# Retention attention and two feed-forward layers: the first four chunks of attention taken as whole chunks, and a new order for the first block

## The chip, the cores and the metric

The kernel runs on one core of a Trainium2 chip. The metric is the device time of one execution in microseconds (us); lower is better. A time is compared with the median of several executions of the kernel before.

## The reference, cut to what matters

```python
scores = scale * np.matmul(q, k.transpose(0, 1, 3, 2))          # B, H, S, D = 4, 8, 576, 64
gamma = 1.0 - 2.0 ** (-5.0 - np.arange(H))
Dmat = np.where(rel >= 0, gamma[:, None, None] ** rel, 0.0)     # rel = query position - key position
x = np.matmul(scores * Dmat, v)                                 # -> x of 2304 tokens x 512
h = x @ moe_w_in;  x = np.maximum(0.01 * h, h) @ moe_w_out      # 512 -> 2048 -> 512
h = x @ moe2_w_in; out = (h * np.cos(h)) @ moe2_w_out
...
```

There is no softmax. The decay is a power of gamma, so that it is split into factors on q, k, v and the result, and what is left of the mask is 0 or 1. Everything is float32.

## The kernel before, in words

**Tiles and stages.** The 2304 tokens are 18 chunks of 128. The feed-forward layers work on blocks of tokens; the first layer has five blocks (512, 512, 512, 384, 384 tokens), and block 0 is chunks 0 to 3. Each product of the feed-forward layers is three products of rounded parts (high times low, low times high, high times high, the type fp32r), so every weight and every input is first split into a high and a low part.

**Weights.** The layer's weights arrive as 64-bit words (1 MB for each of the 16 slices `f` of 128 hidden units) and are turned into float32 by a chain: on ScalarE `abs` (L552) and `lo` (L556), on VectorE `cs` (clamp and shift, two instructions, L560 and L562), `or` (L569) and `add` (L576), then `hi` (ScalarE, L585) and `low` (VectorE, L588). Slice 0 is done in two halves, `a` and `b`.

**Attention.** A chunk's load `ch` (L301) brings q and k transposed by heads, k and v by tokens. `sq` (L315) and `sv` (L327 on VectorE, L322 on ScalarE) scale q and v. Before the change every chunk is done as two halves of 64 tokens: `s` computes k·q within each half (L363), `m` masks it (L384, one VectorE instruction of 128x512), `v` multiplies by the values (L401), `g` makes k times v of each half (L425), `st` adds it to the running state (L449, one per half), `r` multiplies the state before each half by q (L464), and `tk` scales the result into `xr` (L503). Then `xh` and `xl` (L600, L604) split it into high and low, and the first feed-forward matmul can start.

**Feed-forward.** `H0.0` to `H15.3` are the input products of block 0 (L616, 12 matmuls for each of 16 slices), `O0` to `O15` the output products (L630, 12 each). `lk`, `gh`, `gl` (L641, L646, L651) are what lies between. `V3` to `V7` are "visits": the matmuls of attention for the chunks of block 1, put between those of block 0. `~n` are filler matmuls of n times 128 columns, on data that nobody reads (L522).

**What sets the order.** All of block 0 stands in a list written out by hand, `FIRST` (L53 to L71). Each word is a step, and a step's instructions go to their engines' queues in the list's order; each engine (and SyncE's queue of DMA issues, SP) takes its own in that order. All later work has its order in another list, `SECOND`, with the same content before and after. Three loads have an added wait: the first chunk of block 1 (ch4) and slices 2 and 3 wait for chunk 3's `g`, slice 1 and the second half of slice 0 for chunk 1's `s` (`raw()` in `step`, `load_chunk`). With `rows_done` the next group of matmuls in the same banks waits for an empty GpSimd instruction (POOL, L350), which waits for the group before.

Of the kernel before, what the change touches and what calls it, by code (L numbers as in the profile page):

```python
# [68 lines left out]
lk14 gh14 gl14 st8.1 tk7 H15.0 H15.1 H15.2 H15.3 O14 lk15 or15b add15b gh15 gl15 hi15b low15b O15 m8 ch9 sq9
sv9  # L70
# [168 lines left out]
def retention_ffn_ffn(  # L239
# [28 lines left out]
    def scratch(name, shape):  # L268
# [27 lines left out]
    def load_chunk(i):  # L296
        if 2 <= i < n_first:

            ch = w_tile(NF + 1 - i, [P, 4, DM], F32, "ch")
        else:  # L300
            ch = ap.tile([P, 4, DM], F32, tag="ch", name="ch")  # L301
        ch_t[i] = ch
        if i == 0:
            nc.sync.dma_start(ch[:, :2], qkv[i, :2].rearrange("x p d -> p x d"))
            nc.sync.dma_start(ch[:, 2:], qkv[i, 2:].rearrange("x p d -> p x d"))
        else:
            got = nc.sync.dma_start(ch, qkv[i].rearrange("x p d -> p x d"))
            if i == n_first:
                in_turn(got, last_of["grown"])
# [23 lines left out]
    def banks_of(i):  # L333

        if i < n_first:
            b = (6, 4, 0, 2)[i]
            lo, hi = [(b, 0), (b + 1, 0)], [(b, NP * C), (b + 1, NP * C)]
            return lo, hi, lo
# [17 lines left out]
    def scores(i):  # L356
        s, ch = banks_of(i)[0], ch_t[i]
        for p in range(NP):
            for x in range(2):
                for e, r in enumerate(halves):  # L360
# [6 lines left out]
                        start=i < n_first or p == 0 and (e == 0 or i == n_first),  # L367
# [3 lines left out]
                    if i >= n_first and e and ("part", i - 1) in last_of:  # L371
                        in_turn(got, last_of.pop(("part", i - 1)))
                    last_of["pe", i - 1] = got
        last_of["scores", i] = got

    def masks(i):
        b, o = banks_of(i)[0][0]
        if i < n_first:

            pt = w_tile(NF // 2 - 1 - i, [P, 2, NP, C], F32, "p_sb")  # L380
        else:
            pt = ap.tile([P, 2, NP, C], F32, tag="p", name="p_sb", bufs=1)
        p_t[i] = pt
# [6 lines left out]
        if i >= n_first:  # L390
            in_turn(got, last_of["pe", i - 1])

    def values(i):
        v, ch, pt = banks_of(i)[1], ch_t[i], p_t.pop(i)
        first = True
        for p in range(NP):
            for x, tok in enumerate(halves):
                for e, r in enumerate(halves):
# [10 lines left out]
                    if first and i >= n_first:  # L409
# [4 lines left out]
        last_of["values", i] = got  # L414

    def growth(i):
        n, ch = banks_of(i)[2], ch_t[i]
        for p in range(NP):
            for x, tok in enumerate(halves):
                if tokens_of(i)[x] == SUBS - 1:  # L420
                    continue
                for e, r in enumerate(halves):
# [6 lines left out]
                        start=i >= n_first and p == 0 and (x == 0 or i == n_first),  # L429
# [3 lines left out]
        last_of["grown"] = got  # L433
# [19 lines left out]
    def reads(i, part):  # L453
# [3 lines left out]
        for p in range(NP):  # L457
            for e, r in enumerate(halves):
# [15 lines left out]
                if ("st", i) in last_of and i < n_first:  # L474
                    in_turn(last_of["pe", i], last_of.pop(("st", i)))
# [1132 lines left out]
```

## Time and profile before

| what | us |
|---|---|
| median of 3 runs | 829.0 (828.11 to 830.35) |
| profiled execution, its own time | 829.85 |
| its span, first to last instruction | 827.7 |
| TensorE busy in the span | 809.1 (98%) |
| VectorE, ScalarE busy | 643.1 (78%), 540.1 (65%) |
| mean granted TensorE clock | 0.991 |

Times in the rows are microseconds from the span's start. The profiled execution is 0.85 us over the median. Its profile shows the engine's matmul rows (PE) and weight-load rows (PEld) apart; a float32 matmul has two rows of each.

### The profile page before, as it was taken

What the parts mean: (1) busy time and instruction counts of PE and PEld (TensorE: products, weight loads), DVE (VectorE), ACT (ScalarE), POOL (GpSimd) and SP (SyncE); (2) the same over time, 40 slices, a digit from 0 to 9 for tenths busy, and PEclk for the clock granted to TensorE, in tenths of its full rate; (3) what the DMA queues carried; (4) which work ended last, traced back from release to release, by engine and by line L of the source; (5) the groups of instructions that cost most, each with busy time, mean ns of one, the idle gap of its engine ahead of it and who ended that gap; (6) DMA issues with size and microseconds to landing.
All of it is one profiled execution on the core that took longest, in us unless ns stands there. A gap on an engine that the chain in (4) does not pass through costs nothing.

```text
span 827.7 us, 16049 instructions
## 1 busy us (share of the span) xinstructions
PE 809.1 (98%) x6134; PEld 742.6 (90%) x6134; DVE 643.1 (78%) x1148; ACT 540.1 (65%) x1041; POOL 6.1 (1%) x8
## 2 busy tenths in 40 slices
PE   7899999999999999999999989999999999999997
PEld 4678887888888888999999989999899999999997
DVE  5899987888887868777741278798698888888785
ACT  4788866556555556466432488887678876778861
POOL 0000011000000000000000000000000000000000
PEclk8899999999999999999999999999999999999999
DMA  8774616786878677867689287598848896637644
GB/s 322 261 275 153 230 53 204 255 256 211 296 250 252 241 228 255 259 221 223 206 265 406 91 349 283 205 331 308 357 132 295 318 384 266 226 127 274 250 164 168
DMA packets 101308, 203.78 MB, mean 246 GB/s; under 512 B 9072, under 2 KB 54896, under 8 KB 96112
## 3 DMA queue, kind: packets, MB, share of 16 engines
q1 hardware_dynamic: 101088, 202.41, 69.0%
q8 instruction: 48, 0.79, 0.4%
q10 hardware_dynamic: 144, 0.35, 0.2%
q14 instruction: 28, 0.23, 0.1%
HBM read 147.42 MB, written 55.31 MB: 245 GB/s over the span
## 4 chain that ended last, share of the span: by engine, by line
PE 80%; DMA 7%; DVE 6%; issue 3%; ACT 2%; SPq 1%; DVEq 0%; POOLq 0%; ACTq 0%
PE psum L630 20%; PE psum L616 20%; PE psum L1435 19%; PE psum L1263 18%; DMA wp<-wp 3%; DMA ch<-in_qkv 1%; DMA y<-graw 1%; DMA ws<-ws 1%; PE psum L401 1%; DMA raw<-in_w 1%; PE psum L464 1%; PE psum L425 1%; DVE t L569 1%; DVE t L576 1%; DVE w L588 1%
## 5 line engine op out<-in xcount | busy, mean ns | idle before, releaser
L616 PE MATMUL psum<-x_sb,w 128*128 128x512 f32 (+1 forms) x960 | 212.0, 370 | 1.2 <-DVE x_sb L604 0.9
L630 PE MATMUL psum<-g,w 128*128 128x512 f32 (+1 forms) x960 | 211.8, 370 | 0.4 <-DVE graw L873 0.4
L616 PEld LDWEIGHTS psum<-x_sb,w 128*128 128x128 f32 x960 | 174.8, 188 | 26.1 <-DVE x_sb L604 1.6
L630 PEld LDWEIGHTS psum<-g,w 128*128 128x128 f32 x960 | 174.4, 188 | 25.3 <-DVE g L651 1.4
L1263 PE MATMUL psum<-x,ws 128*128 128x384 f32 x576 | 111.3, 337 | 2.8 <-DMA ws<-ws 2.3
L1263 PEld LDWEIGHTS psum<-x,ws 128*128 128x128 f32 x576 | 101.5, 189 | 3.5 <-DMA ws<-ws 2.6
L917 DVE TENSOR_TENSOR g<-graw,g 128x512 fp32r<-128x512 f32 (+1 forms) x64 | 39.7, 623 | 61.0 <-ACT g L914 60.8
L1435 PE MATMUL psum<-g,wp 128*128 128x384 f32 x432 | 83.1, 338 | 2.8 <-DMA wp<-wp 1.9
L1263 PE MATMUL psum<-x,wa 128*128 128x384 f32 x432 | 84.0, 335 | 0.0
L1435 PE MATMUL psum<-g,wq 128*128 128x384 f32 x432 | 80.9, 335 | 0.1
L1435 PEld LDWEIGHTS psum<-g,wp 128*128 128x128 f32 x432 | 75.7, 189 | 4.7 <-DMA wp<-wp 1.9
L1435 PEld LDWEIGHTS psum<-g,wq 128*128 128x128 f32 x432 | 75.2, 188 | 0.9 <-DVE acc L1472 0.7
L1263 PEld LDWEIGHTS psum<-x,wa 128*128 128x128 f32 x432 | 75.7, 188 | 0.0
L910 ACT ACTIVATE graw<-psum 128x512 f32<-128x512 f32 (+1 forms) x64 | 34.7, 542 | 60.7 <-PE psum L616 56.1
L914 ACT CAST g<-graw 128x512 fp32r<-128x512 f32 (+1 forms) x64 | 36.1, 567 | 48.0 <-PE psum L630 47.8
L1472 DVE TENSOR_TENSOR acc<-psum,acc 128x384 f32<-128x384 f32 x90 | 48.3, 553 | 19.9 <-PE psum L1435 19.5
L1312 DVE SCALAR_TENSOR_TENSOR r<-r,h 128x768 f32<-128x768 int32 x48 | 45.6, 954 | 6.8 <-ACT r L1307 6.3
L1293 DVE TENSOR_TENSOR h<-psum,s 128x384 f32<-128x384 f32 x48 | 26.4, 554 | 29.5 <-PE psum L1263 27.0
L1334 DVE TENSOR_TENSOR g<-tq,g 128x768 fp32r<-128x768 f32 x48 | 45.1, 953 | 4.7 <-ACT g L1338 4.5
L1321 DVE SCALAR_TENSOR_TENSOR h<-r,h 128x768 f32<-128x768 f32 x48 | 45.5, 952 | 3.6 <-ACT r L1318 3.4
L1338 ACT CAST g<-tq 128x768 fp32r<-128x768 f32 x48 | 39.8, 835 | 8.0 <-DVE tq L1355 4.9
L1307 ACT CAST r<-h 128x768 int32<-128x768 f32 x48 | 40.2, 837 | 7.1 <-DVE h L1293 5.2
(115 smaller groups left out, 1068.5 us busy)
## 6 DMA issues: line engine op xcount, KB each, us to landing
ws<-ws SPq DMA_DIRECT2D x20, 1024.0 KB, 8.4
wp<-wp SPq DMA_DIRECT2D x20, 1024.0 KB, 7.0
ch<-in_qkv SPq DMA_DIRECT2D x17, 1024.0 KB, 6.4
x<-xq SPq DMA_DIRECT2D x21, 768.0 KB, 7.8
wa<-wa SPq DMA_DIRECT2D x20, 768.0 KB, 6.4
wq<-wq SPq DMA_DIRECT2D x20, 768.0 KB, 7.3
raw<-in_w SPq DMA_DIRECT2D x14, 1024.0 KB, 9.8
mraw<-in_w SPq DMA_DIRECT2D x32, 256.0 KB, 3.4
```

The costliest lines, as they stand in the source:

```text
L616: nc.tensor.matmul(hp, wt[:, i, cols], x_t[lj, k][:, j, :n], start=(k == 0 and a == 0), stop=(k == KK - 1 and a == 2),)
L630: nc.tensor.matmul(psum[:, BANK_O + m, :n], wt[:, i, cols], gt[:, j, :n], start=(f == 0 and a == 0), stop=(f == NF - 1 and a == 2),)
L914: nc.scalar.copy(g.ap[:, 0, :n], y.ap[:, :n])
L917: nc.vector.tensor_tensor(out=g.ap[:, 1, :n], in0=y.ap[:, :n], in1=g.ap[:, 0, :n].bitcast(F32), op=ALU.subtract)
L1263: nc.tensor.matmul(bank[BANKS[m]].rearrange("p (q t) -> p q t", t=Q), a[:, hl, i, j * P : (j + 1) * P], x[:, :, v, j, :], start=m in (1, 5 ...
L1307: "ACT", 885, lambda: nc.scalar.copy(rb.ap.bitcast(I32), pair()),
L1312: nc.vector.scalar_tensor_tensor(out=rb.ap, in0=rb.ap.bitcast(I32), scalar=-1.0, in1=pair(), op0=ALU.mult, op1=ALU.add)
L1321: nc.vector.scalar_tensor_tensor(out=pair(), in0=rb.ap, scalar=0.5, in1=pair(), op0=ALU.subtract, op1=ALU.mult)
L1334: nc.vector.tensor_tensor(out=gb.ap[:, :, 1], in0=src(), in1=gb.ap[:, :, 0].bitcast(F32), op=ALU.subtract)
L1338: h_ = add("ACT", 885 if n == 2 else 515, lambda: nc.scalar.copy(gb.ap[:, :, 0], src()), [*needs, opened["all"]], due, 0, gb.old)
L1435: nc.tensor.matmul(to, wt[:, hl, i, t * P : (t + 1) * P], gt[:, fi, v, :], start=m in (1, 5) and h == 0 and x == 0, stop=h == 1 and x == 2 ...
L1472: x = add("DVE", 560, lambda: nc.vector.tensor_tensor(out=kept(), in0=to, in1=kept(), op=ALU.add), [got], due - SOON / 2)
```

## The change

It does five things. The four chunks of block 0 are no longer done by halves: `whole_scores`, `whole_masks`, `whole_values`, `whole_growth`, `whole_states` and `whole_reads` do 128 tokens at once, with a 128x128 mask of their own in the tables. The three added waits of loads are gone; a load waits for room only. The arrays in memory are laid out by partition, so that a row of a chunk or of a weight slice is 8 KB in one piece (the host's array has another order of the same numbers). The list `FIRST` is another one. The code of the halves stays for chunks 4 to 17.

```diff
@@ FIRST (the first lines of each; the lists go on to H15, O15)
-ch0 sq0 s0 sv0 m0 raw0a abs0a cs0a or0a ~3 v0 g0 st0.0 st0.1 ~4 r0.0 ch1 sq1 s1 r0 lo0a add0a ch2 m1 sq2 sv1
-hi0a low0a v1 g1 s2 st1.0 st1.1 r1.0 sv2 m2 v2 r1 ch3 sq3 sv3 raw0b raw1 tk0 g2 st2.0 st2.1 s3 m3 abs0b tk1
-cs0b or0b lo0b add0b r2.0 r2 v3 g3 st3.0 st3.1 ~5 r3.0 r3 abs1 cs1 or1 lo1 hi0b low0b add1 tk2 tk3 xh0 xl0 xh1
+raw0a abs0a cs0a or0a raw0b abs0b cs0b lo0a add0a or0b ch1 sq1 lo0b add0b ~24 s1 m1 sv1 ~4 g1 hi0a hi0b low0a
+ch0 sq0 s0 v1 sv0 ch2 ch3 raw1 raw2 raw3 m0 ~1 g0 sq2 s2 st0.0 st1.0 m2 sq3 sv2 v0 tk0 r1.0 r1.1 tk1 low0b g2
+st2.0 s3 v2 r2.0 m3 sv3 ~4 g3 r2.1 abs1 cs1 or1 st3.0 lo1 add1 v3 r3.0 r3.1 tk2 tk3 xh0 xl0 xh1 xh2 ~10 H0.0
...
@@ the mask, a column of the tables
+    tabs.append(np.arange(P)[:, None] <= np.arange(P)[None, :])
@@ load_chunk
-            nc.sync.dma_start(ch[:, :2], qkv[i, :2].rearrange("x p d -> p x d"))
-            nc.sync.dma_start(ch[:, 2:], qkv[i, 2:].rearrange("x p d -> p x d"))
+            nc.sync.dma_start(ch[:, :2], qkv[i, :, :2])
+            nc.sync.dma_start(ch[:, 2:], qkv[i, :, 2:])
         else:
-            got = nc.sync.dma_start(ch, qkv[i].rearrange("x p d -> p x d"))
-            if i == n_first:
-                in_turn(got, last_of["grown"])
+            nc.sync.dma_start(ch, qkv[i])
@@ raw() in step
-            got = load_raw(n) if half is None else load_half(0, n, half)
-            if n == 1 or n == 0 and half:
-                in_turn(got, last_of["scores", 1])
-            if n in (2, 3):
-                in_turn(got, last_of["grown"])
+            load_raw(n) if half is None else load_half(0, n, half)
@@ new
+    FIRST_BANK = (6, 4, 0, 2)
+    whole = [slice(p * P, (p + 1) * P) for p in range(NP)]
+    def whole_scores(i):
+        ch = ch_t[i]
+        for p, t in enumerate(whole):
+            for e, r in enumerate(halves):
+                got = nc.tensor.matmul(
+                    psum[:, FIRST_BANK[i] + e, t], ch[r, 1, t], ch[r, 0, t],
+                    start=True, stop=True, skip_group_check=True,
+                )
+    def whole_masks(i):
+        b = FIRST_BANK[i]
+        p_t[i] = pt = w_tile(NF // 2 - 1 - i, [P, 2, NP, P], F32, "p_sb")
+        nc.vector.tensor_tensor(
+            out=pt,
+            in0=psum[:, b : b + 2].rearrange("p e (n c) -> p e n c", n=NP),
+            in1=wide_sb.unsqueeze(1).unsqueeze(1).to_broadcast([P, 2, NP, P]),
+            op=ALU.mult,
+        )
+    def whole_values(i):
+        for p, t in enumerate(whole):
+            for e in range(2):
+                got = nc.tensor.matmul(
+                    psum[halves[e ^ p % 2], FIRST_BANK[i] + 1, t], ch[:, 3, head_of(p, e)], pt[:, e, p, :],
+                    start=p == 0, stop=True, skip_group_check=True,
+                )
+        if i:
+            last_of["rows", i] = rows_done(got)
+    def whole_growth(i):
+        for p in range(NP):
+            for e, r in enumerate(halves):
+                got = nc.tensor.matmul(
+                    psum[r, FIRST_BANK[i], p * D : (p + 1) * D],
+                    ch[:, 2, head_of(p, e)], ch[:, 3, head_of(p, e)],
+                    start=p == 0, stop=True, skip_group_check=True,
+                )
+    def whole_reads(i, e):
+        behind = [last_of.pop(("rows", i))]
+        r = halves[e]
+        for p, t in enumerate(whole):
+            got = nc.tensor.matmul(
+                psum[halves[e ^ p % 2], FIRST_BANK[i] + 1, t], state[2 * i][r, p * D : (p + 1) * D], ch_t[i][r, 0, t],
+                start=False, stop=True, skip_group_check=True,
+            )
+            while behind:
+                in_turn(got, behind.pop())
...
```

Chunk 0 has no `r` any more (its state is empty), each chunk has one `st` instead of two, and of block 1's work `V3` stands behind `O2` instead of ahead of `H3`, with its `sq4`, and `V4` to `V7` one product later.

**What moves on TensorE**, from the filler ahead of the first attention matmuls to the end of chunk 3; psum is the result's bank, ch a chunk, st the state, p_sb the masked scores, tabs_sb and still the filler's data. Before, from chunk 1's later reads to chunk 3's k times v:

```order
L464 MATMUL psum<-ch,st 64x64 x8
L425 MATMUL psum<-ch 64x64 x16
L363 MATMUL psum<-ch 64x64 x16
L464 MATMUL psum<-ch,st 64x64 x16
L401 MATMUL psum<-p_sb,ch 64x64 x16
L425 MATMUL psum<-ch 64x64 x16
L522 MATMUL psum<-tabs_sb,still 128x512
```

After the change, from chunk 2's scores to chunk 3's reads:

```order
L346 MATMUL psum<-ch 128x128 x8
L366 MATMUL psum<-p_sb,ch 64x128 x8
L398 MATMUL psum<-ch,st 64x128 x8
L377 MATMUL psum<-ch 64x64 x8
L346 MATMUL psum<-ch 128x128 x8
L366 MATMUL psum<-p_sb,ch 64x128 x8
L398 MATMUL psum<-ch,st 64x128 x4
L581 MATMUL psum<-tabs_sb,still 128x512
L377 MATMUL psum<-ch 64x64 x8
L398 MATMUL psum<-ch,st 64x128 x4
L366 MATMUL psum<-p_sb,ch 64x128 x8
L398 MATMUL psum<-ch,st 64x128 x8
```

The shape is that of the result. There are half as many matmuls in a group, most with twice the columns, and a filler of 512 columns stands between chunk 2's two groups of reads.

**What moves on SP's queue**, the first loads of the program; raw is a slice of weights, ch a chunk. Before:

```order
L304 DMA ch<-in_qkv 128x2x512
L305 DMA ch<-in_qkv 128x2x512
L539 DMA raw<-in_w 128x2x256
L307 DMA ch<-in_qkv 128x4x512 x3
L539 DMA raw<-in_w 128x2x256
L534 DMA raw<-in_w 128x4x256
L307 DMA ch<-in_qkv 128x4x512
L534 DMA raw<-in_w 128x4x256 x7
```

After:

```order
L598 DMA raw<-in_w 128x512 x2
L306 DMA ch<-in_qkv 128x2048
L303 DMA ch<-in_qkv 128x1024
L304 DMA ch<-in_qkv 128x1024
L306 DMA ch<-in_qkv 128x2048 x2
L593 DMA raw<-in_w 128x1024 x3
L306 DMA ch<-in_qkv 128x2048
L593 DMA raw<-in_w 128x1024 x5
```

Both halves of weight slice 0 come ahead of all chunks, chunk 1 ahead of chunk 0, and slices 2 and 3 ahead of ch4.

**What moves on VectorE**, between chunk 3's mask and the first low part of the input (x_sb); t is a slice of weights in conversion. Before:

```order
L384 TENSOR_TENSOR p_sb<-psum,tabs_sb 128x512
L560 TENSOR_SCALAR t_394<-t_394 128x512
L562 TENSOR_SCALAR t_394<-t_394 128x512
L569 SCALAR_TENSOR_TENSOR t_394<-raw,t_394 128x512
L576 ISA t_394<-raw,t_394 128x1024
L449 TENSOR_TENSOR st<-psum,st 128x256 x2
L560 TENSOR_SCALAR t_477<-t_477 128x1024
L562 TENSOR_SCALAR t_477<-t_477 128x1024
L569 SCALAR_TENSOR_TENSOR t_477<-raw,t_477 128x1024
L588 TENSOR_TENSOR w_242<-t_394,w_242 128x512
L576 ISA t_477<-raw,t_477 128x2048
L604 TENSOR_TENSOR x_sb<-xr,x_sb 128x512 x2
```

After:

```order
L355 TENSOR_TENSOR p_sb<-psum,tabs_sb 128x1024
L324 TENSOR_TENSOR ch<-ch,tabs_sb 128x512
L617 TENSOR_SCALAR t_334<-t_334 128x1024
L619 TENSOR_SCALAR t_334<-t_334 128x1024
L626 SCALAR_TENSOR_TENSOR t_334<-raw,t_334 128x1024
L390 TENSOR_TENSOR st<-psum,st 128x256
L633 ISA t_334<-raw,t_334 128x2048
L661 TENSOR_TENSOR x_sb<-xr,x_sb 128x512 x4
```

The conversion of slice 0 has left this stretch for the program's start, the mask has twice the elements, and the scaling of ch4's q (L315 before, between the x_sb) is gone from between the four low parts.

## Rows read from the trace of the kernel before

**Rows 1.** The page, parts 1 and 2: busy time; 40 equal slices.

```profile
PE 809.1 (98%) x6134; PEld 742.6 (90%) x6134; DVE 643.1 (78%) x1148; ACT 540.1 (65%) x1041; POOL 6.1 (1%) x8
...
PE   7899999999999999999999989999999999999997
```

**Rows 2.** Stretches: TensorE, weight loads, VectorE, ScalarE, GpSimd busy; clock, DMA share, GB/s.

```profile
10.00:14.00 4.00, 2.22 (x50) 1.12 (x49) 3.59 (x7) 2.53 (x9) 0.00 (x0) 1.00 1.05 385
...
15.00:25.00 10.00, 7.95 (x251) 7.06 (x248) 6.59 (x13) 7.45 (x20) 0.00 (x0) 0.50 0.53 192
434.00:440.00 6.00, 6.00 (x37) 6.00 (x36) 1.03 (x2) 1.42 (x3) 0.00 (x0) 1.00 1.01 422
```

**Rows 3.** Timeline of VectorE, 31 to 48 us: start, length, instruction, wait before it.

```profile
31.23 1.28 DVE L604 TENSOR_TENSOR x_sb<-xr,x_sb 128x512 fp32r<-128x512 f32 x2
...
36.00 0.69 DVE L560 TENSOR_SCALAR t<-t 128x1024 f32<-128x1024 f32 x1 [0.54 <-ACT t L552]
...
47.33 1.22 DVE L588 TENSOR_TENSOR w<-t,w 128x1024 fp32r<-128x1024 f32 x1
```

**Rows 4.** Timeline of VectorE, 6 to 11 us.

```profile
6.00 0.69 DVE L315 TENSOR_TENSOR ch<-ch,tabs_sb 128x512 f32<-128x512 f32 x1 [4.46 <-DMA ch<-in_qkv]
...
9.36 0.43 DVE L560 TENSOR_SCALAR t<-t 128x512 f32<-128x512 f32 x1 [0.78 <-ACT t L552]
...
10.28 0.69 DVE L569 SCALAR_TENSOR_TENSOR t<-raw,t 128x512 uint32<-128x512 uint32 x1
10.89 0.42 DVE L447 COPY st<-psum 128x256 f32<-128x256 f32 x1
```

**Rows 5.** Timeline of ScalarE, 8 to 32 us.

```profile
8.64 0.69 ACT L552 ACTIVATE t<-raw 128x512 f32<-128x512 f32 x1 [5.96 <-DMA raw<-in_w]
...
11.41 2.02 ACT L322 ACTIVATE ch<-ch,tabs_sb 128x64 f32<-128x64 f32 x8 [1.50 <-DMA ch<-in_qkv]
...
28.19 1.14 ACT L503 ACTIVATE xr<-psum,tabs_sb 128x128 f32<-128x128 f32 x4 [0.37 <-PE psum L464]
29.20 2.19 ACT L600 CAST x_sb<-xr 128x512 fp32r<-128x512 f32 x4
```

**Rows 6.** Timeline of TensorE, 11 to 38 us.

```profile
11.89 0.45 PE L464 MATMUL psum<-ch,st 64*64 64x64 f32 x8 [1.04 <-DVE st L449]
...
27.66 0.46 PE L464 MATMUL psum<-ch,st 64*64 64x64 f32 x16 [0.15 <-POOLq L350]
28.05 3.06 PE L522 MATMUL psum<-tabs_sb,still 128*128 128x512 f32 x8
31.97 6.37 PE L616 MATMUL psum<-x_sb,w 128*128 128x512 f32 x24 [0.86 <-DVE x_sb L604]
```

**Rows 7.** Timeline of TensorE, 91 to 122 us.

```profile
91.94 2.88 PE L616 MATMUL psum<-x_sb,w 128*128 128x512 f32 x12
94.75 0.69 PE L401 MATMUL psum<-p_sb,ch 64*64 64x64 f32 x32
...
95.97 0.65 PE L363 MATMUL psum<-ch 64*64 64x64 f32 x32
96.43 0.41 PE L464 MATMUL psum<-ch,st 64*64 64x64 f32 x16
96.78 3.01 PE L616 MATMUL psum<-x_sb,w 128*128 128x512 f32 x12
99.62 5.60 PE L630 MATMUL psum<-g,w 128*128 128x512 f32 x24
...
112.76 5.88 PE L630 MATMUL psum<-g,w 128*128 128x512 f32 x24
118.48 2.88 PE L616 MATMUL psum<-x_sb,w 128*128 128x512 f32 x12
121.50 0.69 PE L401 MATMUL psum<-p_sb,ch 64*64 64x64 f32 x32
```

**Rows 8.** Groups by line and shape, weight loads, 32 to 124 us.

```profile
L616 PEld LDWEIGHTS psum<-x_sb,w 128*128 128x128 f32 x183 | 33.8, 188 | 9.4 <-DVE x_sb L604 1.6 <-DVE w L588 0.7
```

More of the change, by code (lines that the diff above doesn't have):

```diff
@@ L276, in retention_ffn_ffn @@
     wq_d = [scratch(f"wq{p}", [P, 2, 3, 2 * P]) for p in range(NPAIR)]
-    sizes = (C, NP * P, (CYCLE + 1) * NP, CYCLE * H)
+    sizes = (C, NP * P, (CYCLE + 1) * NP, CYCLE * H, P)
     tabs_sb = const.tile([P, sum(sizes)], F32, name="tabs_sb")
-    mask_sb, itab_sb, otab_sb, vtab_sb = (
-        tabs_sb[:, sum(sizes[:x]) : sum(sizes[: x + 1])] for x in range(4)
+    mask_sb, itab_sb, otab_sb, vtab_sb, wide_sb = (
+        tabs_sb[:, sum(sizes[:x]) : sum(sizes[: x + 1])] for x in range(5)
     )
@@ L333, in banks_of, with head_of @@
     def banks_of(i):
[L335 to L338, printed above, removed]
         b = BANK_A
         return [(b, 0), (b + 1, 0)], [(b + 1, NP * C), (b + 2, NP * C)], [(b, NP * C), (b + 2, 0)]
+    FIRST_BANK = (6, 4, 0, 2)
+    whole = [slice(p * P, (p + 1) * P) for p in range(NP)]
+    def head_of(p, e):
+        return slice((2 * p + e) * D, (2 * p + e + 1) * D)
+    def whole_scores(i):
[6 more added lines that the diff above has]
+                )
+        last_of["scores", i] = got
@@ new lines, in whole_growth, with whole_states @@
+    def whole_growth(i):
+        ch = ch_t[i]
+        for p in range(NP):
[5 more added lines that the diff above has]
+                )
+        last_of["grown"] = got
+    def whole_states(i):
+        new = ap.tile([P, NP * D], F32, tag="st", name="st", bufs=3)
+        add = psum[:, FIRST_BANK[i], : NP * D]
+        if i == 0:
+            nc.vector.tensor_copy(new, add)
+        else:
+            nc.vector.tensor_tensor(out=new, in0=add, in1=state[2 * i], op=ALU.add)
+        state[2 * i + 2] = new
@@ new lines, in whole_reads @@
+    def whole_reads(i, e):
[8 more added lines that the diff above has]
+                in_turn(got, behind.pop())
+        if not e:
+            last_of["rows", i] = rows_done(got)
@@ L366, in scores @@
                         ch[r, 0, t],
-                        start=i < n_first or p == 0 and (e == 0 or i == n_first),
+                        start=p == 0 and (e == 0 or i == n_first),
                         stop=True,
@@ L370, in scores @@
                     )
-                    if i >= n_first and e and ("part", i - 1) in last_of:
+                    if e and ("part", i - 1) in last_of:
                         in_turn(got, last_of.pop(("part", i - 1)))
                     last_of["pe", i - 1] = got
-        last_of["scores", i] = got
     def masks(i):
         b, o = banks_of(i)[0][0]
[L378 to L383, printed above, removed]
+        p_t[i] = pt = ap.tile([P, 2, NP, C], F32, tag="p", name="p_sb", bufs=1)
         got = nc.vector.tensor_tensor(
@@ L389, in masks @@
         )
-        if i >= n_first:
-            in_turn(got, last_of["pe", i - 1])
+        in_turn(got, last_of["pe", i - 1])
     def values(i):
@@ L408, in values @@
                     )
-                    if first and i >= n_first:
+                    if first:
                         in_turn(got, last_of["st", i])
@@ L428, in growth @@
                         ch[tok, 3, h],
-                        start=i >= n_first and p == 0 and (x == 0 or i == n_first),
+                        start=p == 0 and (x == 0 or i == n_first),
                         stop=True,
@@ L501, in take @@
                 xr[j, p] = xr[1, p] if j > 1 else multi.tile([P, T], F32, tag="xr", name="xr", bufs=4)
+            if i < n_first:
+                last_of["take", i] = nc.scalar.activation(
+                    xr[j, p][:, t0 : t0 + P], psum[:, b, whole[p]], AF.Copy, scale=otab_sb[:, c * NP + p : c * NP + p + 1]
+                )
+                continue
             for x0, x1, t in parts:
```

58 lines of the change are left out of this document (26 added, 32 removed).

## The prediction

> **What bounds the kernel now.** I read the page first. TensorE (PE) is busy 98% of the span, and in the 40 slices every digit from the third on is 9, but for one 8 and the last; only the first two slices, 41 us, have room [rows 1]. So I read that stretch on each engine's timeline. The first feed-forward matmul starts at 31.97 us and waits for VectorE's first low part of the input (x_sb, L604) [rows 6]. After it block 0 has two nearly equal bounds: TensorE, whose 12 matmuls take 2.72 us when nothing is late (24 of them last 5.60, 12 last 2.88 [rows 7]), and VectorE, which needs slice after slice. The reader should see the one place where VectorE decides: the last low part of slice 3 is written at 47.33 to 48.55 [rows 3], and `H3` runs on it. Later small waits remain: 112.76 to 118.48 is 5.72 for 24 where 5.44 would do, and 118.48 to 121.50 is 3.02 where 91.94 to 94.75 is 2.81 [rows 7], 0.5 us in all. A gain is thus an earlier x_sb, less VectorE work between x_sb and slice 3, or less of the 0.5.
>
> Two more views bear on it. From 15 to 25 us the granted clock is 0.50, that is 1.2 instead of 2.4 GHz, after four us (10 to 14) in which TensorE was busy 2.22 [rows 2]. And in those ten us the DMA engines are busy 53% at 192 GB/s: the loads of slices 2 and 3 are waiting for chunk 3. They come late, yet VectorE loses only 0.54 us by it, at 36.00 [rows 3].
>
> **Part 1: the start, up to chunk 2's scores.** Slice 0's first half is now first in the queue. The first load before had the same 512 KB and shared the engines with the tables, and was used at 6.0 [rows 4]; so `abs` starts at 6.0, and VectorE 0.72 later, as 9.36 follows 8.64 [rows 4, 5]. It does both halves of slice 0: two clamps of 0.92 (9.36 to 10.28), two `or` and one `add` of 0.61 (10.28 to 10.89): 6.7 + 3.7 = 10.4. Chunk 1 landed by 11.41 [rows 5] with half a megabyte more ahead of it, 1.36 us at 385 GB/s [rows 2], so it is there at 10.1. `sq` 0.69, then scores at 11.15.
>
> A group's length is the main unknown. Before, a group of 32 rows of 64 columns, four 64x64 tiles at a time, takes 0.46 (95.97 to 96.43) [rows 7]. The row at 11.89 has 8 rows, two tiles side by side, and takes 0.45, as long as the 16 rows at 27.66 that go four at a time [rows 6]. The whole-chunk groups are 16 rows of 128 columns, with half or all of the array's rows per tile, so two at a time: twice 0.46, I take 0.9. The bounds are 0.46 (four's rate after all) and 1.8 (one by one). `g` is 16 rows of 64 columns: 0.47. Each half of `r` is 8 rows of 128: 0.45.
>
> So scores end at 12.2 with 0.15 of latency; mask 1.13 (an instruction of 128x1024 is 1.22 long [rows 3], 0.09 overlap), slice 0's low part 0.61, `sq` of chunk 0: 14.7; scores; mask 0 from 15.85; `sq` of chunk 2: scores of chunk 2 at 17.8. Chunk 2's data is not late: with three megabytes of chunks, one of weights and the tables moved at 385 GB/s it lands near 16.
>
> **Part 2: chunk 2's scores to the input.** From here TensorE's queue is the path. Its groups: s2 0.9, v0 0.9, r1 0.9, g2 0.47, s3 0.9, v2 0.9, half of r2 0.45, the filler 0.85 (1664 columns take 3.06 less 0.2 latency [rows 6], 512 columns 0.85), g3 0.47, the rest of r2 0.45, v3 0.9, r3 0.9: 9.0 us. The filler is on the path, since g3's scaled v is there at 24.8 and TensorE only at 25.7. Four halves of `r` wait for an empty GpSimd instruction, 0.15 [rows 6] plus 0.11 latency: 1.05.
>
> Tile shapes change between groups. The row: 12 matmuls from 91.94 at 2.72 end their turn at 94.66, and the 64x64 group starts at 94.75, 0.09 late, with about 0.05 more before its second four; on the way back 96.78 plus 2.72 is 99.50 and the next starts at 99.62 [rows 7]. I take 0.14 per change, nine changes without another wait: 1.3. Bounds: 0 and 2.2 (0.25 each, both ends counted). The Trainium skill says in TensorEngine Tiling (Array Packing), Key Properties, that changing the tiling mode drains the engine, which speaks against a change that goes from one shape to the next in every group; by that rule alone, without a figure, the sum has such a term, and the trace agrees with the 0.09.
>
> 9.0 + 1.05 + 1.3 + 0.1 of latency puts the end of r3 at 29.3. `tk` 1.0 (28.19 to 29.20), `xh` 0.55 (2.19 for four) [rows 5], and the first low part starts at 31.05 instead of 31.23 [rows 3]. **Gain 0.2.** VectorE's own queue (mask 1.13, `sv` 0.61, two clamps 1.45, `or` 1.2, `st` 0.36, `add` 1.2 from 22.95) would be ready at 28.9, 2.15 earlier: it is not the bound.
>
> **Part 3: the input to slice 3.** The 0.54 wait goes: slice 2 is loaded straight behind slice 1 and lands by 24. `sq4` goes behind slice 3: 0.6 (0.69 in [rows 4], overlapped). VectorE reaches the end of slice 3's low part 0.2 + 0.54 + 0.6 = 1.35 earlier, near 47.2. But `V3` lay ahead of it, in a TensorE wait, and now comes behind: half a `g` 0.24, scores 0.46, two shape changes 0.25: **0.95 given back.** Net 0.4.
>
> **Part 4: the rest.** Of the later 0.5 us of waits, between none and all goes, since VectorE keeps `sq4` to do; I take half, 0.25. Rows of 8 KB move faster (422 GB/s from 434 to 440, where loads have rows of 6 and 8 KB, against 385 [rows 2]), but what they load lands ahead of its use in this walk, so I price that at nothing; if chunks became the bound again, a megabyte would be 0.25 us cheaper. Layer 2's weights are now read as 2 KB pieces of 8 KB rows; they lie under a TensorE that is 98% busy [rows 1], and I price that at nothing too. Later `V`s by one product: same work, nothing.
>
> **Sum:** -0.4 - 0.25 = -0.65 us. The profiled execution, 829.85, would become 829.2; it is 0.85 over the median of the runs, 829.0, and against that median I say **828.4**. 0.3% is 2.5 us, about what a measurement of this kernel can tell from no change, so this is no change. Its own range is 827.0 to 830.5.
>
> **Rivals.** *TensorE's path is shorter.* If changing shapes costs nothing (1.3) and the filler falls into a wait for `sv` (0.85), TensorE is 2.15 us earlier and VectorE's queue, ready at 28.9, becomes the bound: 828.4 - 2.15 = 826.2, and less with the rest of the later waits gone. For it: those are my least certain terms, and a group may overlap the next. Against: the 0.09 at 94.75. Chance 0.32.
>
> *The clock falls.* Before, it fell to 1.2 GHz after 2.22 busy us of 4 and stayed for ten [rows 2]. After the change the idlest four, 13 to 17 us, hold a wait of about 1 us ahead of chunk 0's scores: about 3 of 4. If chunk 0's data or VectorE is half a microsecond later, the fall becomes likely. Ten us in which TensorE, nine tenths busy, goes at half speed put about 4.6 us on the path: 833.0, **slower**. [...] Chance 0.16.
>
> *Weights of full-height tiles are not hidden.* A weight load of 128 columns takes 188 ns [rows 8] and 12 matmuls still go in 2.72, or 227 ns each [rows 7]: those loads, over all rows, are hidden. The Trainium skill (TensorE: Matmul & The Clock Gate, Part 3 on packing small matmuls) says a load overlaps running matmuls only when its row group differs; by that rule `v` and `g`, now over all rows, would pay. Five such groups lie on the path, 8 pairs of loads each, about 0.094 for 64 columns: 3.8 us, 832.2. The rows speak against it; with the case that tiles run one by one, chance 0.08.
>
> That the loads still come late is part of the forecast: it gives back the 0.54 and no more.
>
> **Chances and range.** No change 0.44, faster by over 0.3% 0.32, slower 0.24. The range 825.2 to 833.2 takes in the shorter path with a microsecond more and the clock's fall.
>
> **What would show it.** TensorE's timeline: scores of chunk 2 near 17.8, a group of scores 0.9 from its successor, first feed-forward matmul at 31.8, the low part of slice 3 ended near 47.2. The clock's rows at 1.00 from 10 to 30. No wait for slice 2. The forecast is wrong if the first feed-forward matmul comes before 30 or after 33.5, or if it comes as said and the block's end is over 2 us elsewhere.

## The result, and the profile after

The changed kernel takes **834.12 us** (median of 4, 833.03 to 834.26) against 829.4 of the kernel before on the same chip: ratio 1.0056, 95% interval 1.0037 to 1.0074, so 4.7 us slower. The forecast was no change (828.4, range 825.2 to 833.2). In a second comparison, beside three experiments, the ratio was 1.0094 (1.0068 to 1.0119).

The page of the changed kernel, answering [rows 1], with the granted clock in its last line:

```profile
PE 814.9 (98%) x5888; PEld 743.2 (89%) x5888; DVE 644.7 (78%) x1144; ACT 540.5 (65%) x1041; POOL 6.1 (1%) x8
...
PE   8999999999999999999999999999999999999997
...
PEclk9999999999999999999999999999999999999999
```

The stretches of [rows 2] after the change:

```profile
10.00:14.00 4.00, 4.00 (x23) 1.84 (x21) 2.70 (x5) 3.05 (x10) 0.00 (x0) 1.00 1.03 426
15.00:25.00 10.00, 9.44 (x157) 7.84 (x152) 7.61 (x12) 5.69 (x18) 0.00 (x0) 1.00 1.01 418
```

The clock no longer falls: it is granted at 1.00 (2.4 GHz) where it was at 0.50, and TensorE was busy all of the four microseconds ahead. The DMA engines run at 418 GB/s where they were half idle. Clock and loads are better, and the start is later all the same. TensorE's timeline, answering [rows 6] (L581 filler, L346 scores, L377 k times v, L366 values, L398 state times q, L673 feed-forward):

```profile
6.71 5.39 PE L581 MATMUL psum<-tabs_sb,still 128*128 128x512 f32 x12
12.03 1.16 PE L346 MATMUL psum<-ch 64*128 64x128 f32 x16
...
18.87 1.16 PE L346 MATMUL psum<-ch 64*128 64x128 f32 x16
19.96 1.09 PE L366 MATMUL psum<-p_sb,ch 128*64 128x128 f32 x16
20.99 1.44 PE L398 MATMUL psum<-ch,st 64*64 64x128 f32 x16
22.36 0.69 PE L377 MATMUL psum<-ch 128*64 128x64 f32 x16
...
30.75 2.42 PE L581 MATMUL psum<-tabs_sb,still 128*128 128x512 f32 x6
33.29 4.94 PE L673 MATMUL psum<-x_sb,w 128*128 128x512 f32 x20
```

The first feed-forward matmul comes at 33.29; in [rows 6] it came at 31.97. ScalarE's first `abs` (in [rows 5] at 8.64, behind chunk 0):

```profile
6.43 0.66 ACT L609 ACTIVATE t<-raw 128x512 f32<-128x512 f32 x1 [3.77 <-DMA raw<-in_w]
```

VectorE, answering [rows 3] and [rows 4]:

```profile
10.66 0.69 DVE L312 TENSOR_TENSOR ch<-ch,tabs_sb 128x512 f32<-128x512 f32 x1
...
32.55 2.50 DVE L661 TENSOR_TENSOR x_sb<-xr,x_sb 128x512 fp32r<-128x512 f32 x4 [2.48 <-ACT x_sb L657]
...
47.79 1.22 DVE L645 TENSOR_TENSOR w<-t,w 128x1024 fp32r<-128x1024 f32 x1
```

The first of these is `sq1`, the next the four low parts of the input, the last slice 3's low part. The 0.54 us wait of [rows 3] is gone, and still slice 3's low part starts at 47.79, not 47.33. The 1.3 us by which the first feed-forward matmul is late are the smaller part of the loss. The larger part appears 90 us later. First TensorE of the kernel before, the last products of block 0 and the first of block 1 (L616 input, L630 output products):

```profile
54.05 2.90 PE L616 MATMUL psum<-x_sb,w 128*128 128x512 f32 x12
...
132.12 8.66 PE L616 MATMUL psum<-x_sb,w 128*128 128x512 f32 x36
140.61 2.96 PE L630 MATMUL psum<-g,w 128*128 128x512 f32 x12
```

The same after the change (L673, L687):

```profile
55.69 3.02 PE L673 MATMUL psum<-x_sb,w 128*128 128x512 f32 x12
...
122.76 0.39 PE L673 MATMUL psum<-x_sb,w 128*128 128x512 f32 x1
124.10 2.80 PE L673 MATMUL psum<-x_sb,w 128*128 128x512 f32 x11 [0.95 <-DVE w L645]
127.32 0.69 PE L459 MATMUL psum<-p_sb,ch 64*64 64x64 f32 x32 [0.42 <-ACT xr L562]
...
135.12 0.97 PE L673 MATMUL psum<-x_sb,w 128*128 128x512 f32 x3
136.81 0.96 PE L673 MATMUL psum<-x_sb,w 128*128 128x512 f32 x3 [0.72 <-DVE x_sb L905]
138.26 7.26 PE L673 MATMUL psum<-x_sb,w 128*128 128x512 f32 x30 [0.49 <-DVE x_sb L905]
145.35 0.86 PE L687 MATMUL psum<-g,w 128*128 128x512 f32 x3
```

`H4` is 1.64 us later than before (55.69 against 54.05), the first output product of block 1 is 4.74 later (145.35 against 140.61). So 3.1 us are lost between, in four waits that the kernel before doesn't have: behind `H15`'s first matmul, before `V7`, and twice in block 1's first product. Behind 145 us nothing large is added. (The profiled executions end 3.2 us apart and not 4.7, since the one of the kernel before ran some matmuls near 588 us at half clock.)

Three of the four waits name VectorE; the one before `V7` names ScalarE's `tk` (L562). VectorE's rows, and GpSimd's, at the block's end before the change:

```profile
117.42 1.78 DVE L569 SCALAR_TENSOR_TENSOR t<-raw,t 128x512 uint32<-128x512 uint32 x1
119.12 1.26 DVE L560 TENSOR_SCALAR t<-t 128x512 f32<-128x512 f32 x1
...
131.29 2.57 DVE L852 TENSOR_TENSOR x_sb<-xr,x_sb 128x512 fp32r<-128x512 f32 x4
```

```profile
116.47 2.17 POOL L315 TENSOR_TENSOR ch<-ch,tabs_sb 128x512 f32<-128x512 f32 x1 [116.03 <-DVE t L562]
118.61 1.49 POOL L327 TENSOR_TENSOR ch<-ch,tabs_sb 128x512 f32<-128x512 f32 x1
129.22 1.29 POOL L315 TENSOR_TENSOR ch<-ch,tabs_sb 128x512 f32<-128x512 f32 x1 [9.12 <-DVE w L588]
```

And after it:

```profile
122.34 1.70 DVE L645 TENSOR_TENSOR w<-t,w 128x512 fp32r<-128x512 f32 x1
...
124.30 1.19 DVE L708 TENSOR_TENSOR g<-graw,g 128x512 fp32r<-128x512 f32 x1
...
134.38 4.42 DVE L905 TENSOR_TENSOR x_sb<-xr,x_sb 128x512 fp32r<-128x512 f32 x4
```

```profile
122.21 1.28 POOL L312 TENSOR_TENSOR ch<-ch,tabs_sb 128x512 f32<-128x512 f32 x1 [121.77 <-ACT g L703]
123.46 1.49 POOL L324 TENSOR_TENSOR ch<-ch,tabs_sb 128x512 f32<-128x512 f32 x1
134.53 1.67 POOL L312 TENSOR_TENSOR ch<-ch,tabs_sb 128x512 f32<-128x512 f32 x1 [9.59 <-DVE graw L926]
136.16 1.49 POOL L324 TENSOR_TENSOR ch<-ch,tabs_sb 128x512 f32<-128x512 f32 x1
```

GpSimd's only real work in block 0 is the scaling of chunks 8 and 9 (`sq8 sv8`, `sq9 sv9`). While it runs, VectorE's instructions stretch: a low part of 128x512 takes 1.70 instead of 0.69, the four low parts of block 1's input 4.42 instead of 2.57. The kernel before pays too (1.78 and 1.26 at 117.42 and 119.12), but in this trace it falls on conversions that TensorE doesn't wait for, and chunk 9's scaling on a pause of VectorE and on two instructions that it does not stretch (the mask at 129.08, a copy at 130.69). Each scaling starts when its chunk has landed, and the chunk's load waits for the buffer that a `V` frees. After the change the two loads are issued behind `V6` and `V7`:

```profile
114.67 0.33 SPq L306 DMA_DIRECT2D ch<-in_qkv  x1
129.53 0.33 SPq L306 DMA_DIRECT2D ch<-in_qkv  x1
```

They land 7.3 and 4.8 us later, just ahead of GpSimd's 122.21 and 134.53. Before, the issues were at 110.11 and 123.73, landing 6.1 and 5.3 later. So with the front late and `V4` to `V7` one product later it all comes 5 to 6 us later, under the low parts that TensorE needs next.

### The profile page after: what moved, and what is told of

Same layout as the page of the kernel before. It is cut to its first block, busy times and chain, and to the rows that moved or that the text cites. A ratio compares the mean times of both kernels' runs of the same rounds, so it can differ in the third digit from the quotient of the medians.

```text
span 830.9 us, 15563 instructions
## 1 busy us (share of the span) xinstructions
PE 814.9 (98%) x5888; PEld 743.2 (89%) x5888; DVE 644.7 (78%) x1144; ACT 540.5 (65%) x1041; POOL 6.1 (1%) x8
## 4 chain that ended last, share of the span: by engine, by line
PE 83%; DVE 6%; DMA 5%; ACT 4%; issue 1%; SPq 1%; DVEq 0%; POOLq 0%; ACTq 0%
PE psum L687 20%; PE psum L673 20%; PE psum L1316 19%; PE psum L1488 19%; DMA wp<-wp 2%; DMA ws<-ws 1%; PE psum L581 1%; PE psum L459 1%; DMA ch<-in_qkv 1%; PE psum L575 1%; PE psum L482 1%; PE psum L428 1%; DVE t L633 1%; PE psum L520 1%; DVE w L645 1%
## 5 line engine op out<-in xcount | busy, mean ns | idle before, releaser
L673 PE MATMUL psum<-x_sb,w 128*128 128x512 f32 (+1 forms) x960 | 212.6, 370 | 4.2 <-DVE w L645 1.3
L687 PE MATMUL psum<-g,w 128*128 128x512 f32 (+1 forms) x960 | 211.7, 370 | 0.0
L673 PEld LDWEIGHTS psum<-x_sb,w 128*128 128x128 f32 x960 | 174.6, 188 | 31.0 <-DVE x_sb L905 2.5
L687 PEld LDWEIGHTS psum<-g,w 128*128 128x128 f32 x960 | 174.4, 188 | 23.9 <-DVE g L708 0.4
```

The lines of the kernel that those rows point to most:

```text
L673: nc.tensor.matmul(hp, wt[:, i, cols], x_t[lj, k][:, j, :n], start=(k == 0 and a == 0), stop=(k == KK - 1 and a == 2),)
L687: nc.tensor.matmul(psum[:, BANK_O + m, :n], wt[:, i, cols], gt[:, j, :n], start=(f == 0 and a == 0), stop=(f == NF - 1 and a == 2),)
```

## The experiments

Theory **C**: that collision of GpSimd with VectorE costs 3 of the 4.7 us. Theory **F**: the front's 1.3 us is filler on TensorE's path. Rivals: the front alone (R), the late place of `V7` by itself (L), the whole-chunk groups (W), the rows of 8 KB. The changed kernel itself came to 1.0056 of the kernel before in one comparison and to 1.0094 in another, so a difference of 0.4% or less between kernels measured on different chips says little by itself.

**The block's end.** `e1_old_tail` takes the changed list up to `H4`, then the old order.

```diff
 ... H4.0 H4.1 H4.2 H4.3
-gh3 gl3 O3 ... H9.3 low10 or11 add11 sv5 V4 ... H15.3 sq8 sv8 V7 ... O14 O15 ch9 sq9 sv9
+gh3 gl3 O3 ... H8.2 H8.3 V4 ch6 ... low15a V7 st8.0 ... H15.0 ... O15 m8 ch9 sq9 sv9
```

> The changed kernel up to H4 of its list, then what is left in the order that the list had before the change (V4 to V7 one product earlier, slice 15's parts in their old places). Theory C (late Vs, collision): in the changed kernel V6 at 112.44 and V7 at 127.32 free the chunk buffers late, so GpSimd's scaling of chunks 8 and 9 falls to 122.2 to 125.0 and 134.5 to 137.7, where it stretches VectorE's low part of slice 15a (1.70 instead of 0.69) and the four low parts of block 1's input (4.42 instead of 2.57): 3.0 us of TensorE waits. Undone, the median goes from 834.1 to 831.1 (830.3 to 832.0), the four low parts take 2.6, and no wait over 0.3 stands before H15 and H(1,0). Rival R (the front): all that is late is late because the first input is 1.3 us later, the tail only follows; then 833.4 to 834.6, with the waits near H15 still there.

Measured: 833.14, ratio 1.0063 (1.0048 to 1.0077): no gain that can be told. But the collision stayed; GpSimd and VectorE in its trace:

```profile
117.26 1.40 POOL L312 TENSOR_TENSOR ch<-ch,tabs_sb 128x512 f32<-128x512 f32 x1 [116.82 <-DMA ch<-in_qkv]
```

```profile
117.42 1.52 DVE L617 TENSOR_SCALAR t<-t 128x512 f32<-128x512 f32 x1
...
133.86 3.37 DVE L905 TENSOR_TENSOR x_sb<-xr,x_sb 128x512 fp32r<-128x512 f32 x4
```

So the place of the `V`s alone is not the switch; when the chunk lands against what VectorE is doing is, and the landing is itself 4.8 to 7.3 us behind its issue. The waits fell from 2.6 us in four to 1.0 in two (0.52 and 0.48).

`e2_new_tail` is the mirror: the kernel before, the changed order behind `H4`.

```diff
 ... H4.0 H4.1 H4.2 H4.3
-gh3 gl3 O3 ... H8.2 H8.3 V4 ch6 ... low15a V7 st8.0 ... H15.0 ... O15 m8 ch9 sq9 sv9
+gh3 gl3 O3 ... H9.3 low10 or11 add11 sv5 V4 ... H15.3 sq8 sv8 V7 ... O14 O15 ch9 sq9 sv9
```

> The kernel before up to H4, then what is left in the changed list's order: the tail alone. Theory C: 829.4 + 3.0 = 832.4 (831.5 to 833.2), with a stretched low part of slice 15a or of block 1's input under GpSimd's scaling. Rival R: 828.9 to 830.0, no new wait.

Measured: 828.97, ratio 1.0018 (1.0005 to 1.0031), half of what C expected. Waits of 0.8 in `H15` and 0.4 before `V7` are there, but block 1's low parts take 2.49: in this run they are nearly through when GpSimd starts at 134.86.

`e3_no_scale` takes the cause away.

```diff
     def scale_q(i):
+        if n_busy <= i < n_busy + 2:
+            return
@@ the same in scale_v
```

> The changed kernel without the scaling of chunks 8 and 9 on GpSimd (q and v of these two chunks stay unscaled; this part of the computation is left out), order and all else as changed. Theory C with the price in the collision: the low part of slice 15a takes 0.69, the four low parts 2.6, 834.1 - 3.0 = 831.1 (830.4 to 832.0). Rival L: the late place of V7 costs by itself (take, mask and low parts behind it come late whatever GpSimd does): 833.2 to 834.5.

Measured: 830.59 (10 runs), inside C's range in microseconds; low part of slice 15a 0.68, the four 2.49. But the kernel before took 827.11 beside it, not 829.4: the ratio is 1.0041 (1.0025 to 1.0056), where C's range means 1.0012 to 1.0031, and it is not told apart from the changed kernel's 1.0056. The trace speaks against L: `V7` has the same place in the order, and the four waits are gone.

`e8_apart` leaves nothing out and gives the work to VectorE.

```diff
-        eng = nc.gpsimd if n_busy <= i < n_busy + 2 else nc.vector
+        eng = nc.vector
@@ FIRST: without sq9 sv9; x_low in split_block
+                    if j == 1 and p == KK - 1:
+                        scale_q(n_busy + 1)
+                        scale_v(n_busy + 1)
```

`e5_again` is the changed kernel beside it, on the same chip.

> The changed kernel once more, as the base for the three kernels beside it on the same chip: 1.0056 of the kernel before (1.0037 to 1.0074); TensorE reaches block 1's first matmul at 135.1 and has 1.2 us of waits right behind it. If the 4.6 us that the first trace has at 138 us were chance, they would differ by over 0.5 here.

> The changed kernel with the scaling of chunks 8 and 9 on VectorE instead of GpSimd, chunk 9's behind the last of block 1's four low parts; nothing is left out. Theory C (GpSimd's collision with VectorE is what the block's end costs): the four low parts take 2.6 instead of 4.42, no wait behind block 1's first matmul, the low part of slice 15a 0.69; 2.3 us less, ratio to the kernel before 1.0025 to 1.0035. Rival L (V7's late place): ratio 1.005 or more, the waits stay.

Measured: `e5_again` 835.19, 1.0094, with the same waits as in the first trace. `e8_apart` **831.31**, 1.0042 (1.0026 to 1.0057): 3.9 us less, though VectorE has four instructions of 0.6 more. Its VectorE and TensorE at block 1's start:

```profile
133.39 2.49 DVE L905 TENSOR_TENSOR x_sb<-xr,x_sb 128x512 fp32r<-128x512 f32 x4
```

```profile
134.13 8.18 PE L673 MATMUL psum<-x_sb,w 128*128 128x512 f32 x34
```

No wait is left there. C is shown, in its sign and mechanism: order and loads are the same but for the scaling itself, and the intervals of the two kernels on one chip do not touch (1.0042, up to 1.0057, against 1.0094, from 1.0068 on).

The traces give its size more closely than the medians. From the start of `H4` to the first output product of block 1, with `e8_apart` as the example,

```profile
56.22 3.02 PE L673 MATMUL psum<-x_sb,w 128*128 128x512 f32 x12
...
142.60 2.96 PE L687 MATMUL psum<-g,w 128*128 128x512 f32 x12
```

it takes, in us, in the one trace that there is of each kernel:

| order behind `H4` | scaling on GpSimd | scaling on VectorE or left out |
|---|---|---|
| changed | 89.66 (changed kernel), 89.41 (`e5`), 89.67 (`e4`), 89.74 (`e6`), 89.88 (`e13`) | 86.38 (`e8`), 86.35 (`e3`), 86.41 (`e11`), 86.37 (`e12`), 86.39 (`e14`) |
| changed, front as before | 87.95 (`e2`) | |
| old, changed front | 87.96 (`e1`) | 86.36 (`e15`) |
| old | 86.56 (before), 86.43 (`e7`), 87.48 (`e9`), 88.17 (`e10`) | 86.49 (`e16`) |

With GpSimd's scaling gone, every order takes 86.4: L falls. With it, the order and the moment of landing decide between nothing and 3.5 us, and the old order pays up to 1.7 too.

**The front.** `e4_less_fill` has four fillers of 512 columns ahead of the first scores instead of six, and none ahead of `g3`:

```diff
-... or0b ch1 sq1 lo0b add0b ~24 s1 ... v2 r2.0 m3 sv3 ~4 g3 ...
+... or0b ch1 sq1 lo0b add0b ~16 s1 ... v2 r2.0 m3 sv3 g3 ...
```

> The changed kernel with 16 instead of 24 filler matmuls ahead of the first scores and without the 4 ahead of g3. Theory F (filler lies on TensorE's path to the first input): first scores at 11.3 instead of 12.03 and 1.05 less ahead of g3, first feed-forward matmul at 31.5 instead of 33.29, and 834.1 - 1.8 = 832.3 (831.6 to 833.0). Rival V: VectorE's slices decide from H2 on, the gain is given back in waits at H2 to H4: 833.5 to 834.5 with the first matmul at 31.5 all the same. Rival K: less filler lets the clock fall between 8 and 20 us: granted clock 0.5 there, over 836.

Measured: 832.5, ratio 1.0054 (1.0037 to 1.0071), in F's range by its median, not told apart from the changed kernel by its ratio. The trace tells more:

```profile
11.59 1.16 PE L346 MATMUL psum<-ch 64*128 64x128 f32 x16 [1.02 <-DVE ch L312]
...
31.96 5.86 PE L673 MATMUL psum<-x_sb,w 128*128 128x512 f32 x24
```

The first feed-forward matmul is 1.33 earlier (31.96 against 33.29); of what should come, 1.8, that is three quarters, and block 1's first product still has the lead (133.79 against 135.12). The clock stays at 1.00. V and K fall.

`e6_halves` undoes the whole chunks in the changed order; the sums of the first four chunks come out otherwise in it.

```diff
-            "s": lambda: whole_scores(n),
+            "s": lambda: scores(n),
@@ the same for m, v, g, st, r; in FIRST
-... st2.0 s3 v2 r2.0 ... r2.1 ...
+... st2.0 st2.1 s3 v2 r2.0 ... r2 ...
```

> The changed kernel's loads, rows and order, but the first four chunks in halves of 64 tokens again, as before the change (r0 added behind v0, st in two steps). Theory W (the whole-chunk groups lengthen TensorE's path): scores and values take 0.5 instead of 1.09, the first feed-forward matmul comes near 31.5 instead of 33.3, and the ratio to the kernel before falls from 1.0056 to about 1.0035. Rival S (the halves' chain of state steps between VectorE and TensorE is longer than what the groups save): the first matmul at 34 or later, ratio over 1.006.

Measured: 838.44, ratio 1.0123 (1.0098 to 1.0149). The stretch from 16 to 28 us, and the first feed-forward matmul:

```profile
16.00:28.00 12.00, 8.18 (x245) 7.02 (x248) 5.45 (x11) 5.37 (x15) 0.00 (x0) 0.63 1.00 400
```

```profile
37.30 5.86 PE L611 MATMUL psum<-x_sb,w 128*128 128x512 f32 x24
```

W falls, and S holds: with short groups TensorE waits more (it is busy 8.18 of 12 us), and the clock falls to a mean of 0.63. How much of the loss is the chain of states and how much the clock is not told apart. In this order whole chunks are the better choice.

**The rows.** `e7_rows`, `e9_layer2_rows` and `e10_layer1_rows` put all, layer 2's or layer 1's rows into the kernel before.

```diff
-            got = nc.sync.dma_start(ch, qkv[i].rearrange("x p d -> p x d"))
+            got = nc.sync.dma_start(ch, qkv[i])
@@ the same in load_raw, load_half, layer 2's load and the host's arrays
```

> The kernel before with rows of 8 KB alone (chunks, slices, layer 2's weights in 2 KB pieces of the rows); order, waits and halves as before. Theory F (rows cost nothing later and bring chunks a little earlier): 0.9975 to 1.0000 of the kernel before. Rival P: layer 2's pieces, now with a stride of 8 KB, come later and TensorE waits for them from 200 us on: over 1.002, with waits on DMA in the trace that the kernel before doesn't have.

> The kernel before, with only layer 2's weights stored in rows of 8 KB and read as pieces of 2 KB out of them; chunks and layer 1's slices as before. Theory P (the 0.33% that the rows cost lies in these pieces): 1.0025 to 1.0040 of the kernel before. Rival Q (it lies in chunks and layer 1's slices): 0.9990 to 1.0010.

> The kernel before, with chunks and layer 1's slices in rows of 8 KB and layer 2's weights packed as before. Theory P: 0.9985 to 1.0010 of the kernel before. Rival Q: 1.0025 to 1.0040.

Measured: 1.0033 (1.0019 to 1.0048), 1.0013 (0.9995 to 1.0031) and 1.0019 (1.0001 to 1.0037). The rows cost 2.5 us in the kernel before, so F falls. The halves add up to it, but each lies between P's range and Q's, and neither is clear alone. Of the waits that e7's rival P expects, none is seen between 200 and 480 us. The trace of e10 shows the collision in the order of before:

```profile
132.95 1.29 POOL L315 TENSOR_TENSOR ch<-ch,tabs_sb 128x512 f32<-128x512 f32 x1 [10.97 <-ACT x_sb L846]
```

```profile
133.15 4.29 DVE L850 TENSOR_TENSOR x_sb<-xr,x_sb 128x512 fp32r<-128x512 f32 x4
```

**Both cures, and the rows taken back.** `e11_apart_less` is e8 and e4 together; `e12_packed` packs layer 2 as before; `e13_old_rows` and `e14_cures_old_rows` have all rows as before, without and with the cures; `e15_old_order` is e14 with the old order behind `H4`; `e16_before_apart` is the kernel before with e8's edit.

```diff
@@ e13, e14
-            nc.sync.dma_start(ch, qkv[i])
+            nc.sync.dma_start(ch, qkv[i].rearrange("x p d -> p x d"))
@@ the same in load_raw, load_half, layer 2's load (e12: there alone) and the host's arrays
```

> The changed kernel with both cures: the scaling of chunks 8 and 9 on VectorE (e8_apart, 1.0042), and 16 instead of 24 filler matmuls ahead of the first scores and none ahead of g3 (e4_less_fill took 1.3 us off the first feed-forward matmul). If both add up: 1.0042 - 1.3 / 828 = 1.0026 (1.0015 to 1.0035), first matmul near 32.0, no wait over 0.3 in block 1's first product. Rival V (VectorE bounds the block, the front's gain is lost by H4): 1.0040 or more.

> As e11_apart_less, and layer 2's weights packed as before the change. Theory P: another 0.3% less than e11, 0.9990 to 1.0005 of the kernel before. Rival Q: as e11 within 0.1%.

> The changed kernel with all rows as before the change (chunks, slices and layer 2 packed in 2 KB rows); whole chunks, list and loads that wait for room only stay. Theory R (the rows cost 0.3% here too, as 1.0033 in e7_rows): the changed kernel's 1.0094 to 1.0056 falls by 0.003: 1.0030 to 1.0060. Rival N (in the changed kernel the rows cost nothing, since its loads depend on their speed): 1.0060 to 1.0110, with the first feed-forward matmul later than 34.

> e11_apart_less (both cures) with all rows as before the change. Theory R: 1.0026 - 0.0033 = 0.9993 of the kernel before (0.9980 to 1.0005). Rival N: 1.0020 or more, first matmul over 33.

> As e14, with the list behind H4 in the order of before the change. With GpSimd's scaling gone, theory C expects the order of the tail to be worth little by itself: within 0.1% of e14. Rival L (the place of V4 to V7 costs by itself): 0.2% or more under e14.

> The kernel before with the scaling of chunks 8 and 9 on VectorE, chunk 9's behind the last low part of block 1's input. Theory C: before the change the collision was under other waits (1.78 and 1.26 us at 117.42 and 119.12, none at block 1's start), so little is gained: 0.9980 to 1.0005. Rival: VectorE's 2.4 us more in block 0 and at the start of block 1 decide: over 1.0010.

| kernel | median, us | ratio to before | interval |
|---|---|---|---|
| e11, both cures | 829.81 | 1.0026 | 1.0012 to 1.0040 |
| e12, and layer 2 packed | 828.30 | 1.0001 | 0.9986 to 1.0017 |
| e13, changed, all rows old | 832.96 | 1.0044 | 1.0027 to 1.0062 |
| **e14, cures and all rows old** | **826.31** | **0.9959** | 0.9943 to 0.9976 |
| e15, and old order | 826.38 | 0.9964 | 0.9943 to 0.9985 |
| e16, before, scaling on VectorE | 827.44 | 0.9974 | 0.9961 to 0.9988 |

The cures add up as expected (e11). e12 and e13 lie in the ranges of P and R. With the rows taken back the kernel beats both (e14: 0.41% under before), by more than R expected. The old order adds nothing once GpSimd is out of it (e15), so L falls a second time. And e16 is more than C expected: the kernel before had a collision to lose as well. So of the 3.9 us that e8 takes off the changed kernel, the kernel before could have had some 2 by its median, and the collision alone does not make up the whole difference between the two. Part of what the rows cost is seen by ScalarE's first `abs` and TensorE's first feed-forward matmul, of e11:

```profile
6.80 0.68 ACT L609 ACTIVATE t<-raw 128x512 f32<-128x512 f32 x1 [4.14 <-DMA raw<-in_w]
```

```profile
32.15 5.87 PE L673 MATMUL psum<-x_sb,w 128*128 128x512 f32 x24
```

and of e14:

```profile
5.58 0.67 ACT L611 ACTIVATE t<-raw 128x512 f32<-128x512 f32 x1 [2.90 <-DMA raw<-in_w]
```

```profile
30.97 5.88 PE L675 MATMUL psum<-x_sb,w 128*128 128x512 f32 x24
```

The very first load is there 1.2 us earlier with rows cut in 2 KB pieces (5.58 against 6.80), though from 15 to 25 us the rows of 8 KB move 419 GB/s against 386; and those 1.2 us go straight through to the first feed-forward matmul. In the changed kernel the filler hides this: e13's `abs` starts at 5.73 against 6.43, and its first feed-forward matmul still comes at 33.44 (33.29).

## Why the prediction was wrong, step by step

- **Part 4 is the step that failed: the rest of block 0 behind `H4`, with "Later `V`s by one product: same work, nothing"**. The forecast had a gain of 0.25 there; the runs show 3.1 us lost, to a term that the sum does not have: GpSimd's scaling of chunks 8 and 9 against VectorE. The work is the same, but a `V` frees the buffer for a chunk's load, the load's landing starts GpSimd, and GpSimd stops VectorE. With the scaling on VectorE the same order loses nothing (86.4 us from `H4`, against 89.4 to 89.9). The later `V`s are only part of the trigger: in the kernel before they cost 1.5 us (e2), and with the `V`s back in their places 1.6 us of the collision stay (e1). I followed the `V`s on TensorE only, and not past SP's queue to GpSimd's rows at 116.47 and 129.22, which the trace of before shows with VectorE's stretched 1.78 beside them. The Trainium skill states the rule (SBUF — State Buffer, Who interferes with whom): a VectorE instruction with two inputs in SBUF contends with a GpSimd instruction that reads SBUF, and the ports that they share are an exclusive lock. The trace agrees: of 1.70 us at 122.34, 1.0 is wait, about what GpSimd's instruction of 122.21 to 123.49 had left.
- **Part 1 left out the filler ahead of `s1`.** I had scores at 11.15, behind `sq1`; `sq1` was done at 11.3, but the filler `~24` ran to 12.1. It starts at 6.71, behind the matmuls on zeros that TensorE does from 1.45 on; the tables do not set it, since in e13 they landed by 4.9 and it started at 6.73 all the same. That is 0.9 of the 1.07 by which chunk 2's scores were late (18.87 against 17.8). The `abs` came at 6.43, not 6.0: a cost of the rows (5.73 in e13), hidden here.
- **The group lengths of Part 2 were close.** 18.87 to the end of the last reads at 30.75 is 11.9 against 11.5. Scores are 1.09 from their successor (0.9 was said), values 1.03, k times v 0.62 (0.47), the pair of `r` 1.37 (0.9 and a GpSimd wait of 0.26), the filler 1.05 (0.85 was said, and its own row gives 0.88). What I priced as nine shape changes, 1.3, lies in these lengths. The bounds 0.46 and 1.8 held it.
- **The first feed-forward matmul at 33.29** was inside my bound (30 to 33.5), 1.5 later than 31.8, by the two points above.
- **Part 3 held on VectorE.** From the first low part to the end of slice 3's: 16.5 us (32.55 to 49.01), forecast 16.15; the 0.54 wait and `sq4` went as said. On TensorE 33.29 to `H4` at 55.69 is 22.40, where 31.8 and a net gain of 0.4 make 21.85: another 0.55 of the front's loss.
- **Rows at nothing (Part 4) failed** by 2.5 us in the kernel before (e7). I let their speed speak (422 against 385 GB/s) and did not ask when the first load lands. Where the 2.5 us lie is open.
- **The rivals.** The clock did not fall (1.00 throughout), so my slower rival came out on the right side for the wrong reason. The shorter path of TensorE did not come. Weights of full-height tiles: a group of values takes 1.03, not the 0.9 plus 0.75 that this rival reckons, and no more than a group of scores (1.09), whose weights have half the height. So the loads are hidden but for a tenth. The Trainium skill's rule that I set against it (TensorE: Matmul & The Clock Gate, Part 3) would have them paid; the measurement decides.

Open: where the rows' 2.5 us lie in the kernel before. Its trace with the rows (e7) has block 1's first output product at 140.67, against 140.61 without, so not ahead of that. In the cured kernel 1.2 us are at the first load; e12 against e11 puts 1.5 us on layer 2's pieces, on one chip and with intervals that touch, while e9 gives 0.0013 with an interval that holds zero. That the kernel before's own spread (825 to 833 over all comparisons) comes from the collision is argued, not shown: the four traces of the old order with GpSimd's scaling differ by 1.7 us behind `H4`, and with the scaling on VectorE twelve runs lie within 825.86 to 829.71 (e16), where the kernel before beside them went from 825.57 to 832.71.

## What to carry to other kernels

A step that is moved takes along what it frees: follow the buffer to the load, the landing, and the engine that wakes on it, and look what that engine stops. An engine that is busy 1% of the span (6.1 us) can cost half of that (3.1 us) if it holds another up at the place where the end is set. And a faster stream of loads is not an earlier first load.

## What was not expected of the hardware

- GpSimd's two instructions of some 1.3 to 1.7 us per chunk stretch VectorE's 0.69 to 1.70 and its four low parts from 2.49 to 4.42; not all kinds: the mask at 129.08 and a copy out of PSUM at 130.69, each 0.69 long, ran beside GpSimd unstretched in the kernel before.
- Loads with rows of 4 and 8 KB moved 418 GB/s from 15 to 25 us, those of 2 KB 385 from 10 to 14 [rows 2], and still the first half megabyte was used 0.7 to 1.2 us later.
- A whole-chunk group, with fewer and longer matmuls, goes with a granted clock of 1.00 from 10 to 25 us, where the halves in the same order, with TensorE busy 8.18 of 12 us, got a mean of 0.63 from 16 to 28.
